# Other positions for the pieces of a chunked recurrence, and the weights' low parts all on VectorE

## The chip, the core and the metric

The kernel runs on one core of a Trainium2 chip. A core has five engines that run their own instruction streams side by side: PE (TensorE, matrix products), DVE (VectorE), ACT (ScalarE), POOL (GpSimd) and SP (SyncE, which only issues transfers here). The time is the device time of one execution in microseconds (us); of several runs the median counts. Before the change: median 640.99 us of 3 runs (640.5 to 645.92).

## The reference

Two parts follow each other. The first is a recurrence over 768 time steps, for 4 batches, 8 heads and a head size of 40, with a 40x40 state per head:

```python
for t in range(S):
    y[:, :, t] = np.einsum('bhd,bhde->bhe', rt, state)
    Sa = np.einsum('bhde,bhe->bhd', state, at)
    state_decay = state * wt[:, :, None, :] - np.einsum('bhd,bhe->bhde', Sa, bt)
    state = state_decay + np.einsum('bhd,bhe->bhde', vt, kt)
```

The second is an MLP on y, with heads side by side as x (4, 768, 320): h = gelu(x @ w_in); its two halves of 512 are u and v; v is normalised over its 512 columns and scaled by g_ln; v_s = w_sg @ v + b_sg mixes the 768 time steps; the result is x + (u * v_s) @ w_out. All is fp32.

## The kernel before

**Chunks.** The 768 steps are cut into 12 chunks c of 64, and each chunk into two halves f of the batches and heads. Inside a chunk the recurrence is a triangular system. What doesn't depend on the state is done ahead:

- *The gate* (gate_1 to gate_n): VectorE scans the decays (ex), makes at and, from a scan and a reciprocal, kb; PE turns kb over (kt, copied by ACT to kbt) and multiplies at with kb (ab); VectorE masks ab (at), ACT copies the negated part to nts.
- *The inversion* (inv_load, inv_in, inv_sub, inv_end, inv_turn, inv_back, inv_g, inv_x), once for several chunks: POOL substitutes row by row (tg, x), VectorE ends it (x), transposes (x1z, xt, n), PE and ACT form gp, gs, xp.

What depends on the state is the *chain*, for each c and f: chain1 (ru), chain2 (us), chain_t (tp), chain_u (ut), chain3 (sp, the new state), chain4 (pq) and chain5 (yp, the output), each with its post piece on VectorE or ACT (post1 rhsb, post2 vu, post3 sp and sc, post4 pqs, post5 yt). store5 writes yt out, load_main, load_vb (v, the tile vs), load_rv (rt and vut) fetch for a later chunk.

**Weights.** w_in is used as a high and a low fp32r part. The twelve weight steps k make these in six parts each: 0 loads (stg), 1 takes the size (ACT), 2 and 3 form the scale (DVE), 4 the parts (ACT: one Activate and the cast to wvh or wuh), 5 the low part, three tensor_tensor operations whose last writes wvl or wul. Part 5 is on POOL for the steps k in DECG, else on VectorE:

```python
steps[k] = self.split64(*self.weights_in()[k], HF // 2, self.G if k in DECG else self.V)
```

**Fillers.** While the chunks run, the v half of the MLP's first product is already made for finished time steps: fill_x (loads xf), fill_split (ACT, xfh), fill_low (POOL), fill_v (PE, hf), fill_out (ACT copies hv, SP stores it to hd). load_h reads it back later.

**What sets the order.** Each of these pieces has a position, a number worked out from tables at the head of the program: GATE, GATE0, CHAIN, CHAIN0, YC, YG, INV, BACK, BACK0 for the attention, MAIN_GAP and RV_GAP for the loads, DEC for the weights, FILL for the fillers, PF for reading v back. in_order (L128) sorts all pieces by position and holds a piece back only if a PSUM bank of its ring of six isn't free; then the pieces are issued in that order, each engine in its own queue, and no engine leaves its order. All instructions are issued by one helper, so that every row of the profile says L207. What starts when is decided on the chip, by semaphores. A position is no time: a table entry matters only where two pieces on the same engine change places.

After the chunks comes the MLP proper, batch by batch, up to the end.

Of the kernel before, what the change touches and what calls it, by code (L numbers as in the profile page):

```python
# [43 lines left out]
PER = 25.258  # L44
LATE = 2.5
STORE = 1.5
MAIN_GAP = (3.823, 5.231)
RV_GAP = (1.429, 5.124)
GATE = ((-101.908, -100.107, -99.028, -96.184, -97.801, -95.604, -92.188, -90.251, -93.577, -91.478, -91.765),
    (-93.068, -92.176, -89.578, -85.892, -88.462, -84.822, -80.052, -78.616, -83.325, -79.617, -81.192))  # L50
GATE0 = {(0, 0): (-50.0, (0, 0.6, 1.2, 2.0, 2.1, 3.5, 5.0, 6.2, 6.1, 10.6, 7.4)), (0, 1): (-43.168, (-4.513, -1.768,
# [6 lines left out]
CHAIN = ((-0.122, 2.573, 2.346, 4.973, 4.791, 6.367, 14.029, 15.925, 17.635, 7.581, 9.16, 11.953, 14.479, 16.712,  # L58
    19.293), (10.765, 12.016, 2.382, 3.709, 12.847, 14.479, 15.198, 19.282, 26.19, 15.086, 19.937, 24.082, 25.956,
    28.774, 31.466))  # L60
YC = (6.033, 31.49, 75.962, 101.266, 126.664, 152.164, 177.592, 203.193, 228.664, 254.164, 279.909, 305.328)
YG = (45.508, 65.508, 85.4, 105.4, 126.723, 152.223, 177.723, 203.223, 228.723, 254.223, 280.52, 303.785)
GATEE = {}
GROUPS = ((0,), (1,), (2, 3), (4, 5), (6, 7), (8, 9), (10, 11))
LAST = 2
NBANK = 6
INV = (-61.391, -53.031, -52.526, 0.739, -5.821, -4.877)
INV0 = {0: (-39.357, -31.7, -29.5, 0.443, -3.788, -2.8), 1: (-3.842, -2.4, -0.439, 0.265, 24.398, 26.261), 2: (19.888,
    26.888, 28.456, 0.0, 70.088, 70.788)}
CHAIN0 = {(0, 0): (0.0, 1.942, 2.468, 5.095, 5.152, 6.489, 14.151, 16.047, 17.757, 8.655, 9.521, 12.185, 14.84,  # L70
# [6 lines left out]
BACK0 = {0: (-2.477, -2.272, 2.034, -1.241, 0.905, 2.425, 4.594), 1: (-3.032, -0.637, -0.655, -1.796, -0.68, 1.87,  # L77
    4.322), 2: (-3.032, -0.036, -0.536, -1.677, 0.469, 1.989, 5.535)}
SUBV = ()
N2 = (1, 3)  # L80
KB = 2
BACK = (-4.003, -1.954, -2.561, -3.786, -2.662, 0.399, 2.058)
END_GT = 227.015
END_IW = 274.738
END_RING = 286.936
# [3 lines left out]
PIN = 227.025  # L89
DSTEP = ((-8.5, -1.0, 0.0, 0.7, 1.4, 2.4), (-8.5, -1.0, 0.0, 0.7, 1.4, 2.4))  # L90
DSTEPF = (-9.0, -0.5, 0.0, 0.7, 1.4, 2.4)
DEC = (10.0, 22.0, 34.0, 46.0, 58.0, 72.837, 235.802, 236.543, 248.778, 254.633, 260.025, 266.234)
GE = "VV"
FILL = ((-10.518, -5.255, 1.182, 5.082, 8.462), (3.438, 13.076, 15.947, 19.922, 22.61))
FILLG = True
LASTF = 5
PX = 309.28
# [1 line left out]
PV = 287.036  # L99
PS = 333.785  # L100
PL = 326.785
PF = (302.234, 311.634, 315.428, 323.94, 327.057)
PH = 9
FILLERS = ("v0", "v1", "v2", "v3", "v4")
FIRSTS = ("u1", "u0", "v0", "v1", "u2", "v2", "u3", "v3", "v4", "v5", "u4", "u5", "u6", "u7")
# [1 line left out]
    "v5", "o3", "o5", "o4", "u2", "u3", "u4", "u5", "u7", "u6")  # L107
SEQ_LAST = ("s1", "s2", "s0", "s3", "s4", "s5", "o0", "s6", "s7", "o1", "o2", "o3", "o5", "o4")
XS = 0
DECG = (1, 4)  # L110
DECE = "GGGGGGGG"
DENSE = 1000
DSTEPJ = (-1.1, 0, 0.2, 0.4, 0.6, 0.9)
# [107 lines left out]
def attention(tc, a, xd, flag, keep, ps, mlp=None):  # L221
# [4 lines left out]
    with ExitStack() as ctx:  # L226
# [419 lines left out]
        def at_(p, f, *args, **kw):  # L646
            pieces.append((p, f, args, kw))
# [9 lines left out]
        for c in range(NCH):  # L657
            for f in range(2):
                y, n = GATE0.get((c, f)) or (YG[c], GATE[f])
                at_(y + n[0], gate_1, c, f, 0)  # L660
# [10 lines left out]
                for h in range(2):  # L671
                    at_(y + n[5] + LATE + (MAIN_GAP[f] if h and c > 1 else 0), load_main, 2 * c + f + 2, h)
                z, n = YC[c], CHAIN0.get((c, f), CHAIN[f])
                for g, p in zip((chain1, post1, chain_t, post_t, chain2, post2, chain3, post3, copy3, chain_u, post_u, chain4, post4, chain5, post5), n):
# [4 lines left out]
                for x in range(2):  # L679
                    at_(z + n[13] + LATE + (RV_GAP[f] if x else 0), load_rv, c + 1, f, x)  # L680
            z = YC[c]
            for (g, *k), p in zip(((inv_back, 0), (inv_back, 1), (inv_back, 2), (inv_g,), (post_g,), (inv_x,), (post_x,)), BACK0.get(c, BACK)):
                at_(z + p, g, c, *k)
        for g in GROUPS:
            z, v = (0, INV0[g[0]]) if g[0] in INV0 else (YC[g[0]], INV)
            at_(z + v[0], inv_load, g)
# [39 lines left out]
class Mlp:  # L726
# [345 lines left out]
    def side(self):  # L1072

        def at(p, f, *args):
            plan.append((p, f, args))
# [5 lines left out]
        def wstep(k, i):  # L1081
            if i == 0:
                steps[k] = self.split64(*self.weights_in()[k], HF // 2, self.G if k in DECG else self.V)
            steps[k][i]()

        for k, p in enumerate(DEC):
            for i, d in enumerate(DSTEPF if k < 6 else DSTEP[k % 2]):
                at(p + d if k < 6 else max(PIN + 0.1, p + d), wstep, k, i)
        for k in range(LASTF):
            for b in range(B):  # L1090
                for f, p in zip((self.fill_x, self.fill_split, self.fill_low, self.fill_v, self.fill_out), FILL[1 - b % 2]):
                    n = 2 * k + 2 + (b + 1) // 2
                    at(YC[min(n, NCH - 1)] + PER * max(0, n - NCH + 1) + p, f, b, k)
        at(PO, self.open_out)
# [18 lines left out]
        at(PS, self.split_x, 0, 1)  # L1113
        for k, p in enumerate(PF[:LASTF]):
            at(p - PH, self.load_h, 0, k)
# [177 lines left out]
```

## Time and profile before

| | |
|---|---|
| median of 3 runs | 640.99 us |
| the profiled execution | 640.75 us, its span 639.0 us |
| mean granted clock of PE | 0.886 |
| PE busy | 537.8 us (84%) |
| DVE busy | 494.5 us (77%) |
| ACT busy | 368.9 us (58%) |
| POOL busy | 372.6 us (58%) |
| read from and written to HBM | 54.86 MB, 13.11 MB |

The span runs from the first to the last instruction of the profiled execution. No engine is busy throughout: each stage has its own limit, and so the share of a whole span says little. Roughly, the program is getting ready and inverting for chunk 0 until 62 us, is in chunks 0 to 2 until 160 us, in chunks 3 to 11 until about 390 us, and in the MLP from then on. Rows of a timeline give the start, the duration, the engine, the operation, the tile written and the tiles read with their forms, how many instructions stand together in the row, and in brackets the idle time before it with what ended that. "issue" there means that the engine waited for nothing the profile shows.

### The profile page before, as it was taken

The numbers are of one execution on the slowest core, as the hardware profiler recorded it, in microseconds if no ns is written. First come the engines' busy times: TensorE is split into PE (matmuls) and PEld (weight loads), VectorE is DVE, ScalarE is ACT, GpSimd is POOL, SyncE is SP. The second block draws the span as 40 slices with busy tenths as digits, with TensorE's granted clock in tenths as the row PEclk, the third lists the DMA queues.
The fourth block names the chain that finished last, engine by engine and source line by source line (L and its number), as shares of the span: only waits on it lengthen the run. The fifth ranks groups of instructions, "written<-read, shape, count | busy, mean of one in ns | idle before, by whom it ended". The sixth has DMA issues, their size and how long they took to land.

```text
span 639.0 us, 24143 instructions
## 1 busy us (share of the span) xinstructions
PE 537.8 (84%) x10158; PEld 487.1 (76%) x10158; DVE 494.5 (77%) x948; ACT 368.9 (58%) x817; POOL 372.6 (58%) x606
## 2 busy tenths in 40 slices
PE   6338876867998979889888897798999997999896
PEld 5228765766887868778777786688998997999796
DVE  7768899798688857878799655667689699788833
ACT  2334867367787876788767777365255334424510
POOL 3485858818856980895798443647443634533421
PEclk7758779668999997999988798698999999999899
DMA  6543335343454643542454455245014231512001
GB/s 195 142 115 98 102 77 124 83 125 90 118 141 134 166 127 93 137 134 86 125 144 122 116 155 145 87 126 181 27 59 147 76 118 39 186 57 75 19 12 56
DMA packets 56862, 69.63 MB, mean 109 GB/s; under 512 B 23752, under 2 KB 41800, under 8 KB 54728
## 3 DMA queue, kind: packets, MB, share of 16 engines
q1 hardware_dynamic: 56744, 67.99, 37.5%
q8 instruction: 82, 1.34, 1.0%
q14 instruction: 36, 0.29, 0.2%
HBM read 54.86 MB, written 13.11 MB: 106 GB/s over the span
## 4 chain that ended last, share of the span: by engine, by line
PE 39%; DVE 33%; ACT 9%; issue 9%; DMA 3%; POOL 3%; SPq 2%; ACTq 0%; DVEq 0%; POOLq 0%
PE sg L207 8%; DVE v L207 4%; PE yp L207 4%; PE kt L207 4%; PE ab L207 3%; PE hf L207 3%; DVE fixed L207 3%; PE op L207 3%; PE pq L207 2%; DVE p L207 2%; ACT nts L207 2%; DVE g L207 2%; PE sp L207 2%; DVE kb L207 2%; DVE stg L207 2%
## 5 line engine op out<-in xcount | busy, mean ns | idle before, releaser
L207 POOL TENSOR_TENSOR tg<-x,n 128x135 f32<-128x135 f32 (+25 forms) x203 | 104.5, 515 | 86.3 <-DVE n L207 62.7
L207 POOL TENSOR_TENSOR x<-x,tg 128x135 f32<-128x135 f32 (+25 forms) x203 | 108.8, 536 | 15.9
L207 PE MATMUL sg<-wsh,vh 128*128 128x384 f32 x192 | 64.4, 346 | 10.2 <-ACT wsh L207 3.6
L207 PE MATMUL sg<-wsl,vh 128*128 128x384 f32 x192 | 64.0, 351 | 0.1
L207 PE MATMUL sg<-wsh,vl 128*128 128x384 f32 x192 | 63.8, 351 | 0.0
L207 ACT ACTIVATE nts<-ab 32x512 f32<-32x512 f32 x96 | 46.4, 483 | 21.4 <-PE ab L207 20.1
L207 PE MATMUL kt<-ident,kb 128*128 128x128 f32 x192 | 35.5, 335 | 27.1 <-DVE fixed L207 19.4
L207 POOL TENSOR_TENSOR gx<-g,gy 128x384 fp32r<-128x384 f32 x30 | 31.5, 1060 | 40.5 <-ACT gy L207 40.5
L207 POOL TENSOR_TENSOR rs<-rs,mhalf 128x1 f32<-128x1 f32 x24 | 14.6, 614 | 66.9 <-DVE rs L207 66.9
L207 DVE TENSOR_TENSOR at<-ab,mask 64x512 f32<-64x512 f32 x48 | 31.9, 677 | 26.8 <-ACT nts L207 19.3
L207 PEld LDWEIGHTS kt<-ident,kb 128*128 128x128 f32 x192 | 26.3, 170 | 31.6 <-issue 25.5
L207 ACT CAST vh<-v 128x512 fp32r<-128x512 f32 x24 | 14.6, 619 | 57.7 <-DVE v L207 57.7
L207 PEld LDWEIGHTS sg<-wsh,vh 128*128 128x128 f32 x192 | 36.1, 190 | 12.9 <-ACT vh L207 5.2
L207 ACT CAST gy<-g 128x384 fp32r<-128x384 f32 x30 | 15.4, 513 | 50.7 <-DVE g L207 48.0
L207 PE MATMUL ab<-at,kb 64*64 64x64 f32 x1536 | 37.3, 255 | 8.6 <-DVE fixed L207 6.0
L207 PEld LDWEIGHTS ab<-at,kb 64*64 64x64 f32 x1536 | 32.9, 166 | 12.7 <-issue 8.5
L207 PE MATMUL yp<-pqs,kbt 128*64 128x64 f32 x768 | 35.9, 262 | 3.5 <-DVE pqs L207 3.3
L207 DVE SCALAR_TENSOR_TENSOR g<-sg,gl,bt 128x384 f32<-128x384 f32 x32 | 19.6, 612 | 24.4 <-PE sg L207 13.9
L207 PEld LDWEIGHTS sg<-wsh,vl 128*128 128x128 f32 x192 | 38.2, 200 | 0.0
L207 PE MATMUL pq<-rt,vut 40*64 40x64 f32 x1536 | 33.0, 231 | 6.1 <-ACT vut L207 3.8
L207 PEld LDWEIGHTS sg<-wsl,vh 128*128 128x128 f32 x192 | 37.8, 198 | 0.4 <-DVE wsl L207 0.4
L207 PEld LDWEIGHTS yp<-pqs,kbt 128*64 128x64 f32 x768 | 32.1, 173 | 7.0 <-DVE pqs L207 4.1
(161 smaller groups left out, 1577.2 us busy)
## 6 DMA issues: line engine op xcount, KB each, us to landing
main<-main SPq DMA_DIRECT2D x44, 321.4 KB
hd<-hv SPq DMA_DIRECT2D x20, 256.0 KB
v<-hd SPq DMA_DIRECT2D x20, 256.0 KB
vs<-vb SPq DMA_DIRECT2D x24, 160.0 KB
rt<-rt SPq DMA_DIRECT2D x48, 80.0 KB
vut<-vt SPq DMA_DIRECT2D x48, 80.0 KB
xd<-yt SPq DMA_DIRECT2D x96, 40.0 KB
ws<-seq_w SPq DMA_DIRECT2D x20, 192.0 KB
```

Of the source, the lines that this page charges most:

```text
L207: return self.tc.keep_in_program_order(f(*a, **k))
```

## The change

Position tables take other values, and DECG is empty, so that the low parts of weight steps 1 and 4 are made by VectorE and no longer by POOL. No instruction is added or left out otherwise, and no size changes. The diff, cut to the tables by which most of the moves come about:

```diff
-MAIN_GAP = (3.823, 5.231)
-RV_GAP = (1.429, 5.124)
+MAIN_GAP = (5.4, 4.3)
+RV_GAP = (1.75, 1.2)
...
-YG = (45.508, 65.508, 85.4, 105.4, 126.723, 152.223, 177.723, 203.223, 228.723, 254.223, 280.52, 303.785)
+YG = (45.508, 65.508, 85.508, 105.508, 126.831, 152.331, 177.831, 203.331, 228.831, 254.331, 279.831, 305.331)
...
-BACK = (-4.003, -1.954, -2.561, -3.786, -2.662, 0.399, 2.058)
+BACK = (-4.003, -1.37, -2.126, -3.202, 0.204, 0.399, 2.642)
...
-DEC = (10.0, 22.0, 34.0, 46.0, 58.0, 72.837, 235.802, 236.543, 248.778, 254.633, 260.025, 266.234)
+DEC = (10.0, 22.0, 34.0, 46.0, 58.0, 72.658, 235.802, 242.234, 248.778, 254.446, 260.025, 266.234)
...
-FILL = ((-10.518, -5.255, 1.182, 5.082, 8.462), (3.438, 13.076, 15.947, 19.922, 22.61))
+FILL = ((-10.151, 1.572, 2.299, 5.449, 8.327), (3.438, 13.076, 15.947, 19.922, 22.61))
...
-PF = (302.234, 311.634, 315.428, 323.94, 327.057)
+PF = (302.802, 308.64, 314.802, 323.685, 326.802)
...
-DECG = (1, 4)
+DECG = ()
```

GATE, GATE0, CHAIN, CHAIN0, YC, INV and BACK0 change in the same manner. In the listings that follow, a row is an instruction (or several alike, xN) in the order in which its engine gets it, and a number behind a name only tells one tile from the next.

PE in chunk 0, where the change has the chain's second sp and the ab of gate (3, 1) in another order. Before:

```order
 L207 MATMUL sp<-vu_125,kbt_104 64x40 x16
 L207 MATMUL ab_1153<-at_144,kb 64x64 x2
 L207 MATMUL ab_1154<-at_144,kb 64x64 x2
...
 L207 MATMUL sp<-vu_126,kbt_105 64x40 x16
 L207 MATMUL ut<-ident,vu_126 104x64 x8
```

With the change:

```order
 L207 MATMUL sp<-vu_125,kbt_104 64x40 x16
 L207 MATMUL sp<-vu_126,kbt_105 64x40 x16
 L207 MATMUL ab_1171<-at_144,kb 64x64 x2
 L207 MATMUL ab_1172<-at_144,kb 64x64 x2
```

The second sp moved in front of all of ab; nts on ACT reads ab.

VectorE, a little later, between the end of inversion 1 (x<-x,n) and the first scan (ex) of gate (4, 0); yt is the output of chunk 0's first half, stg and wvl belong to weight step 1:

```order
 L207 SCALAR_TENSOR_TENSOR x<-x,n 128x15 x2
 L207 SCALAR_TENSOR_TENSOR x<-x,n 128x16
+L207 TENSOR_TENSOR stg_1227<-stg_1227,stg_1207 128x256
+L207 TENSOR_TENSOR stg_1008<-stg_1008,wvh 128x256
+L207 TENSOR_TENSOR wvl<-stg_1008,stg_1227 128x256
 L207 SCALAR_TENSOR_TENSOR ex_135<-main_94,fixed_92 128x260
 L207 TENSOR_TENSOR yt<-yp_1231,ex_127 128x4x64
 L207 TENSOR_TENSOR yt<-yp_1232,ex_127 128x4x64
```

The three operations of the low part were POOL's before. The three of weight step 4 come to VectorE in the same way, behind the scans of gate (5, 1) and in front of the two at of gate (5, 0). POOL's queue loses six instructions and is otherwise as it was in these places.

PE in chunk 1, from xp of the inversion to us of the first half. Before:

```order
 L207 MATMUL xp<-xt_97,gs_117 32x32 x32
 L207 MATMUL yp_1552<-pqs,kbt_105 64x64 x2
 L207 MATMUL yp_1553<-pqs,kbt_105 64x64 x2
...
 L207 MATMUL tp<-ident,sc_119 128x128 x4
 L207 MATMUL kt_1588<-ident,kb 128x128 x4
 L207 MATMUL kt_1589<-ident,kb 128x128 x4
 L207 MATMUL tp<-ident,sc_118 128x128 x4
 L207 MATMUL us_1626<-rhsb_115,xt_97 64x40
```

With the change:

```order
 L207 MATMUL xp<-xt_97,gs_117 32x32 x32
 L207 MATMUL tp<-ident,sc_118 128x128 x4
 L207 MATMUL tp<-ident,sc_119 128x128 x4
 L207 MATMUL kt_1575<-ident,kb 128x128 x4
 L207 MATMUL kt_1576<-ident,kb 128x128 x4
 L207 MATMUL yp_1591<-pqs,kbt_105 64x64 x2
 L207 MATMUL yp_1592<-pqs,kbt_105 64x64 x2
```

yp moved behind both tp and both kt. On VectorE the matching yt moved behind the low part of weight step 2. There are more moves of this sort. On VectorE, yt of chunk 1's second half now stands between the two scans of gate (5, 0), and the low part of weight step 6 stands in front of step 7's size, fields and scale. On PE, in chunks 3 to 7, kt of gate (c+3, 1) goes in front of gp, and in chunks 3 to 11 the second sp goes in front of chain_u (ut). On ACT, in chunks 3 to 11, the copies xt and kbt go in front of gs, and step 7's size and parts go behind rhsb and vu of chunk 8's second half. On SP, the second half of a load of main goes behind load_vb, load_rv of the next chunk's second half goes right behind store5 and ahead of the fillers' store, and load_h comes earlier.

## Rows read from the trace of the kernel before

**Rows 1.** Busy time by stretches: each engine (rows), granted clock, DMA share, GB/s.

```profile
84.50:107.60 23.10, 15.68 (x444) 13.50 (x440) 22.67 (x42) 16.74 (x40) 17.06 (x31) 0.78 0.41 102
121.60:137.50 15.90, 9.60 (x256) 8.42 (x252) 14.98 (x35) 6.96 (x14) 8.28 (x15) 0.71 0.46 121
...
222.00:248.00 26.00, 20.24 (x561) 18.17 (x560) 15.92 (x34) 16.15 (x37) 15.56 (x27) 0.80 0.37 94
326.00:352.00 26.00, 21.55 (x567) 18.70 (x556) 25.05 (x50) 19.35 (x48) 21.94 (x35) 0.87 0.42 121
```

**Rows 2.** Timeline of PE in chunks 4 and 6: start, us, instructions, idle before.

```profile
197.77 0.58 PE L207 MATMUL xp<-xt,gs 64*32 64x32 f32 x43 [1.08 <-issue]
...
240.02 0.86 PE L207 MATMUL sp<-vu,kbt 128*64 128x40 f32 x11 [4.41 <-issue]
```

**Rows 3.** The page's DMA queues: packets, MB, share of 16 engines.

```profile
q8 instruction: 82, 1.34, 1.0%
```

**Rows 4.** Timeline of PE in chunk 0, 80 to 83 us.

```profile
80.68 1.16 PE L207 MATMUL ab<-at,kb 64*64 64x64 f32 x64
81.77 1.13 PE L207 MATMUL sp<-vu,kbt 128*64 128x40 f32 x32
```

**Rows 5.** Timeline of ACT, 81 to 85 us.

```profile
81.88 1.99 ACT L207 ACTIVATE nts<-ab 32x512 f32<-32x512 f32 x4 [1.34 <-PE ab L207]
...
84.84 0.40 ACT L207 CAST wvh<-stg 128x256 fp32r<-128x256 f32 x1
```

**Rows 6.** Timeline of VectorE at 84 us.

```profile
84.49 0.69 DVE L207 TENSOR_TENSOR_SCAN ex<-main,fixed 128x260 f32<-128x260 f32 x1
```

**Rows 7.** Tile stg, VectorE's low parts: least, median, longest duration in ns.

```profile
L207 DVE TENSOR_TENSOR stg<-stg,stg x4: 372/416/562, 69.4 to 144.4; 128x256 f32<-128x256 f32 x4
L207 DVE TENSOR_TENSOR stg<-stg,wvh x4: 464/732/904, 69.9 to 144.7; 128x256 f32<-128x256 f32 x4
L207 DVE TENSOR_TENSOR wvl<-stg,stg x4: 424/646/759, 70.5 to 145.2; 128x256 fp32r<-128x256 f32 x4
```

**Rows 8.** Timeline of POOL: where it takes up work after a pause.

```profile
90.59 0.64 POOL L207 TENSOR_TENSOR tg<-x,n 128x31 f32<-128x31 f32 x1 [3.34 <-DVE call L207]
...
144.64 0.24 POOL L207 TENSOR_TENSOR tg<-x,n 128x31 f32<-128x31 f32 x1 [13.06 <-DVE n L207]
```

**Rows 9.** Timeline of PE in chunk 1, 96 to 102 us.

```profile
96.96 1.44 PE L207 MATMUL yp<-pqs,kbt 128*64 128x64 f32 x32
...
101.09 0.66 PE L207 MATMUL kt<-ident,kb 128*128 128x128 f32 x4 [0.15 <-ACT xt L207]
```

**Rows 10.** Timeline of VectorE in chunk 1, 100 to 133 us.

```profile
100.75 0.73 DVE L207 TENSOR_TENSOR yt<-yp,ex 128x256 f32<-128x256 f32 x2
...
118.63 1.27 DVE L207 TENSOR_TENSOR_SCAN ex<-main,fixed 128x260 f32<-128x260 f32 x2
121.62 0.76 DVE L207 TENSOR_TENSOR yt<-yp,ex 128x256 f32<-128x256 f32 x2 [1.72 <-PE yp L207]
...
131.37 0.68 DVE L207 TENSOR_TENSOR at<-ab,mask 64x512 f32<-64x512 f32 x1 [0.32 <-ACT nts L207]
132.22 0.76 DVE L207 TENSOR_TENSOR yt<-yp,ex 128x256 f32<-128x256 f32 x2 [0.17 <-PE yp L207]
```

**Rows 11.** Timelines of VectorE and ACT in chunk 8, 313 to 315 us.

```profile
313.20 0.50 DVE L207 TENSOR_SCALAR cv<-stg 128x256 int32<-128x256 int32 x1
314.06 0.93 DVE L207 TENSOR_SCALAR cv<-cv 128x256 f32<-128x256 f32 x2 [0.35 <-ACT cv L207]
...
314.83 0.42 ACT L207 ACTIVATE cv<-cv 128x256 f32<-128x256 int32 x1
```

**Rows 12.** Groups by line: busy us, mean ns, idle before with its releasers.

```profile
L207 PE MATMUL gp<-x1z,nts 64*32 64x32 f32 x768 | 9.9, 203 | 4.9 <-DVE x1z L207 3.9 <-DVE at L207 0.6 <-issue 0.3
```

**Rows 13.** Timeline of ACT in chunk 4, 193 to 196 us.

```profile
193.25 1.49 ACT L207 COPY gs<-gp 32x256 f32<-32x256 f32 x4 [0.99 <-PE gp L207]
...
195.41 0.76 ACT L207 COPY kbt<-kt 128x320 f32<-128x320 f32 x2
```

More of the change, by code (lines that the diff above doesn't have):

```diff
@@ L46 @@
 STORE = 1.5
-MAIN_GAP = (3.823, 5.231)
-RV_GAP = (1.429, 5.124)
-GATE = ((-101.908, -100.107, -99.028, -96.184, -97.801, -95.604, -92.188, -90.251, -93.577, -91.478, -91.765),
-    (-93.068, -92.176, -89.578, -85.892, -88.462, -84.822, -80.052, -78.616, -83.325, -79.617, -81.192))
-GATE0 = {(0, 0): (-50.0, (0, 0.6, 1.2, 2.0, 2.1, 3.5, 5.0, 6.2, 6.1, 10.6, 7.4)), (0, 1): (-43.168, (-4.513, -1.768,
[6 rows of a table removed]
[L58 to L61, printed above, removed]
-YG = (45.508, 65.508, 85.4, 105.4, 126.723, 152.223, 177.723, 203.223, 228.723, 254.223, 280.52, 303.785)
+MAIN_GAP = (5.4, 4.3)
+RV_GAP = (1.75, 1.2)
+GATE = ((-101.908, -100.107, -99.028, -96.184, -97.801, -95.604, -92.188, -90.251, -93.577, -91.478, -91.823),
+    (-93.163, -92.271, -89.673, -85.987, -88.462, -85.151, -80.147, -78.616, -83.325, -79.712, -81.287))
+GATE0 = {(0, 0): (-50.0, (0, 0.6, 1.2, 2.0, 2.1, 3.5, 5.0, 6.2, 6.1, 10.6, 7.4)), (0, 1): (-43.168, (-2.368, -1.768,
[6 rows of a table added]
+CHAIN = ((-0.122, 1.82, 2.346, 4.973, 4.791, 6.367, 14.029, 15.925, 17.635, 7.581, 9.16, 12.063, 14.479, 16.712,
+    19.293), (10.879, 12.452, 2.818, 4.145, 13.283, 14.157, 15.198, 18.064, 26.304, 15.522, 18.922, 24.082, 26.07,
+    28.888, 30.883))
+YC = (6.033, 31.49, 75.962, 101.266, 126.664, 152.164, 177.592, 203.366, 228.664, 254.164, 279.909, 305.328)
+YG = (45.508, 65.508, 85.508, 105.508, 126.831, 152.331, 177.831, 203.331, 228.831, 254.331, 279.831, 305.331)
 GATEE = {}
@@ L66 @@
 NBANK = 6
-INV = (-61.391, -53.031, -52.526, 0.739, -5.821, -4.877)
+INV = (-61.319, -53.011, -50.525, 0.759, -5.801, -4.857)
 INV0 = {0: (-39.357, -31.7, -29.5, 0.443, -3.788, -2.8), 1: (-3.842, -2.4, -0.439, 0.265, 24.398, 26.261), 2: (19.888,
@@ L76 @@
     15.32, 18.186, 26.426, 16.386, 18.934, 24.094, 26.082, 28.9, 30.895)}
-BACK0 = {0: (-2.477, -2.272, 2.034, -1.241, 0.905, 2.425, 4.594), 1: (-3.032, -0.637, -0.655, -1.796, -0.68, 1.87,
-    4.322), 2: (-3.032, -0.036, -0.536, -1.677, 0.469, 1.989, 5.535)}
+BACK0 = {0: (-2.477, -2.272, 2.034, -1.241, 0.905, 2.425, 4.594), 1: (-3.032, -0.637, -0.655, -1.796, 0.425, 1.87,
+    3.993), 2: (-3.032, -0.036, -0.536, -1.677, 0.469, 1.989, 5.535)}
 SUBV = ()
```

18 rows, old and new, of tables (CHAIN0, GATE0) are left out of this document.

## The prediction

> **What bounds the kernel.** I read the busy table by stretches first, then the timelines of the engines that are full in them, then the tile view of the low parts, and last the waits that the profile names "issue". Up to about 62 us POOL's first inversion sets the pace, and from 435 us the MLP runs in an order that the change leaves alone; I put both at zero. Chunks 0 to 2 (78 to 160 us) are bound by VectorE: it is busy 22.67 of 23.10 us in one stretch and 14.98 of 15.90 in another [rows 1]. There every microsecond put on VectorE comes out at the end, unless a wait of VectorE takes it up. Chunks 3 to 10 repeat every 25 to 26 us, and PE is stopped now and then by waits that no engine ends, named "issue": 1.08 us in front of an xp, and once 4.41 us in front of an sp [rows 2], in a stretch whose granted clock is 0.80 [rows 1] (full speed, 1, is 2.4 GHz, and the lower level 1.2). I read these waits as instruction fetch: the queue that carries instructions as its kind moves 1.34 MB in 82 packets [rows 3], which is 16 KB each, and the long wait comes right behind a burst of loads. Last, 326 to 352 us is full on VectorE again, 25.05 of 26 us [rows 1].
>
> **The sum** is made against the profiled execution, 640.75 us (span 639.0); the median of the three runs shown is 640.99, so 0.2 us above.
>
> *Term 1, the low part of weight step 1, +2.8.* Its three operations go from POOL to VectorE, between the end of inversion 1 and the gate scan ex that now starts at 84.49 [rows 6]. The second of them reads wvh, and ACT's cast of it ends at 84.84 + 0.40 = 85.24. That cast stands behind the nts copies, which waited 1.34 us for PE's ab [rows 5]. PE now runs the second sp in front of this ab. That sp takes 1.13 us as a row, 1.1 with the rows' overlap [rows 4], so nts and cast come 1.1 later, and the cast ends at 86.3. Behind it two operations remain. Their least durations are 0.464 and 0.424 us, their medians 0.73 and 0.65, their longest 0.90 and 0.76 [rows 7]. I take the least, because POOL has nothing to do there until 90.59 (3.34 us of idle) [rows 8], and the slow end I lay to work beside POOL. So ex starts at 86.3 + 0.46 + 0.42 = 87.2 in place of 84.49: 2.7, and 2.8 with a hand-over. Bounds: 1.3 (three least durations, 0.372 + 0.464 + 0.424, no wait) and 3.5 (86.3 + 0.90 + 0.76 against 84.49). POOL gains nothing, since it stands idle behind the three anyway.
>
> The Trainium skill (SBUF — State Buffer, "SBUF: two separate sides") has VectorE and GpSimd share a pair of ports that one of them holds for a whole instruction while the other blocks. The spread from 0.46 to 0.90 us in rows 7 would fit that. By that rule alone, operations that each meet one of POOL's would be at the slow end, and the sum 0.7 us higher; it would be the fast end where POOL is idle.
>
> *Term 2, yp behind kt in chunk 1, +0.5.* PE now does both tp and both kt before this yp. The second kt starts at 101.09 and leaves PE half a microsecond later (0.66 as a row, pipelined), about 101.6; then yp, 1.44 us [rows 9], ends at 103.0. Now yt starts at 100.75, takes 0.73 [rows 10], and the low part of weight step 2 follows it, 1.8 by the medians [rows 7], up to 103.3. After the change the low part goes first and yt waits for yp: 103.0 + 0.73 = 103.75, 0.5 later. Bounds 0 (kt goes earlier) and 0.9 (all of us, behind yp, is late, and with it the next chain).
>
> *Term 3, the scans split by yt, +0.6.* Two scans ex (1.27 us) run together at 118.63, after which VectorE waits 1.72 us for yp until 121.62 [rows 10]. After the change one of them stands behind this yt, so half of 1.27 us leaves the idle time and lands on the path. Bounds 0 and 0.64.
>
> *Term 4, the low part of weight step 4, +0.7.* Three operations come in front of two at. The cast they need is done by then, and POOL is idle there until 144.64 (13.06 us) [rows 8], so they cost their least, about 1.2 [rows 7]. Two waits behind them take some up: 0.32 in front of the second at, 0.17 in front of yt [rows 10]. 1.2 − 0.5 = 0.7. Bounds 0 and 1.7 (1.8 by the medians, nearly nothing absorbed).
>
> *Term 5, weight steps 6 and 7, +1.2.* Now VectorE waits 0.35 us at 314.06 for step 7's size and goes on with that step; the product of step 6 comes later. After the change step 6 is finished first. VectorE is free at 313.20 + 0.50 = 313.7, but the product reads what ACT writes in the row at 314.83, up to 315.25 [rows 11]. Step 7's copy in front of that row goes away, but hv, which waits for PE, stands between, so I leave the row where it is. That is 1.55 us of waiting in place of 0.35, and the stretch behind is full [rows 1]. Bounds 0 (the 0.95 us free in 326 to 352 and slack in front take it) and 2.0 (a second such wait for step 7's parts).
>
> *Term 6, the steady chunks, 0.* In each, kt moves in front of gp, and ACT's copies xt, kbt, xt in front of gs. gp waits 3.9 us in all for x1z [rows 12], so kt can win at most that. Against it gs, now 193.25 to 194.74, comes behind three copies of which the kbt one takes 0.76 us [rows 13], some 2 us, and ends near 196.7. There xp is stopped by "issue" until 197.77 anyway [rows 2]: that wait covers both the gain and the loss. If that cover is gone, gs is later by more than kt is earlier, and each even chunk loses some tenths. Bounds −3.9 and +7 (rival (b)). The moves on SP's queue (main's second halves behind the load of v, rt and vut of the next chunk behind a store) leave each load in front of its first reader, as far as I could follow them; they can act by the burst alone, which is a rival.
>
> Sum: 2.8 + 0.5 + 0.6 + 0.7 + 1.2 + 0 = 5.8; 640.75 + 5.8 = **646.6 us**. All lower ends of terms 1 to 5 give +1.3, all upper ends +8.7, so this case's own range is 642 to 650.
>
> **Rivals.**
> (a) *Not slower: the 4.41-us wait goes.* Main's second half is loaded in the middle of the burst in front of it, and now comes behind the load of v. What decides is whether PE's next 16 KB arrive before PE runs dry, that is a wait near 240 us of under about 0.5. Gain: 4.4 us, and of the slow clock at most 0.20 × 26 = 5.2 more, of which I count half: 7. 646.6 − 7 = 640. For it: the place of the move. Against: the burst's bytes are the same.
> (b) *A second such wait.* The steady chunks have similar bursts, and one of them stopped PE for long, so a new order may as well make another: 646.6 + 7 = 653.6.
> (c) *kt in front of gp pays*, gs hidden: 646.6 − 3.9 = 642.7.
> (d) *The wait goes and VectorE's waits take up most of the additions*: 640.75 + 1.3 − 7 = 635, less with (c).
> The Trainium skill (Runtime: NRT & Kernel Launch, "Instruction fetch mechanics") says that an engine's program is refilled in blocks of 16 KiB by its sequencer's own queue, and that crossing a block is mostly hidden. The block size agrees with rows 3. By "mostly hidden", (a), (b) and (d) would have no cause and the sum would stand; the 4.41 us without a releaser speak against it here.
>
> **How the numbers follow.** Forecast 0.50, (a) 0.22, (b) 0.19, (c) 0.05, (d) 0.04. One per cent, about what a measurement of this kernel can tell from no change, is 634.6 to 647.4 around 640.99. The forecast lies just inside: of its 0.50 I put 0.28 inside and 0.22 above. Nearly all of (a), 0.21, and (c) are inside: same 0.54. Slower: 0.22 + 0.19 = 0.41. Faster: (d) and a tail of (a), 0.05. The range 637 to 654 takes in (a), (b) and (c) and leaves out (d) and the tails.
>
> **What the profile after would show.** Term 1: VectorE idle some 1.7 us until ACT's wvh, then operations of about 0.4 us, ex near 87.2. Term 2: yt waiting for PE's yp, some 3 us later than 103.0. Term 3: one ex before, one behind yt. Term 4: a low part in front of at, and no wait at at. Term 5: VectorE idle 1.2 to 1.6 us on ACT's cv. Term 6: gp with less wait for x1z, xp waiting for gs or "issue" in each even chunk. So chunk 2 should begin 4.6 us later than now, and the rest arise past 310 us. The prediction is wrong if the steady period changes: one long "issue" wait more or less weighs as much as all terms together.

## The result and the profile after

The change made the kernel slower by 0.59%: the ratio to the kernel before is 1.0059, 95% interval 1.0038 to 1.0081, or 3.8 us (2.4 to 5.2) of 641. The medians of 20 runs each are 643.36 us (640.76 to 649.25) and 641.22 (636.91 to 653.02). The forecast was 646.6, within 637 to 654. Single executions of one kernel scatter by several microseconds, and the profiled one of after is a long one, 647.37 us; the profile of before was an average one. So this pair of traces differs by 6.6 us, more than the kernels do. A second trace of each kernel follows further down; where it differs, the text says so.

| | before | after |
|---|---|---|
| profiled execution, its span | 640.75, 639.0 us | 647.37, 645.7 us |
| mean granted clock | 0.886 | 0.876 |
| DVE busy, instructions | 494.5 us, 948 | 496.5 us, 954 |
| POOL busy, instructions | 372.6 us, 606 | 368.7 us, 600 |

The stretches that answer to [rows 1] (same columns; the limits are set where the same work stands in the later trace):

```profile
84.50:112.20 27.70, 18.19 (x509) 16.14 (x499) 25.36 (x51) 19.36 (x44) 14.81 (x28) 0.72 0.32 84
126.00:141.00 15.00, 8.82 (x200) 7.78 (x200) 14.58 (x33) 6.67 (x14) 6.72 (x14) 0.66 0.40 98
...
222.00:250.00 28.00, 24.62 (x751) 21.88 (x753) 18.47 (x39) 20.60 (x46) 18.84 (x32) 0.88 0.45 124
330.00:356.00 26.00, 21.21 (x536) 18.55 (x536) 24.12 (x46) 18.35 (x46) 21.88 (x34) 0.80 0.43 127
```

VectorE is no longer full in the first stretch: 2.3 us are idle in it. In the third the granted clock is 0.88 where it was 0.80. Both are places that the prediction named.

**Term 1.** Timelines of PE, ACT and VectorE of after, which answer to [rows 4], [rows 5] and [rows 6]; the last line is VectorE's x in the trace of before:

```profile
80.69 3.09 PE L207 MATMUL sp<-vu,kbt 128*64 128x40 f32 x64
83.70 1.16 PE L207 MATMUL ab<-at,kb 64*64 64x64 f32 x64
...
84.90 1.97 ACT L207 ACTIVATE nts<-ab 32x512 f32<-32x512 f32 x4 [3.34 <-PE ab L207]
...
87.83 0.40 ACT L207 CAST wvh<-stg 128x256 fp32r<-128x256 f32 x1
...
85.41 0.69 DVE L207 SCALAR_TENSOR_TENSOR x<-x,n 128x15 f32<-128x15 f32 x3
87.96 0.43 DVE L207 TENSOR_TENSOR stg<-stg,stg 128x256 f32<-128x256 f32 x1 [1.86 <-ACT stg L207]
88.30 0.42 DVE L207 TENSOR_TENSOR stg<-stg,wvh 128x256 f32<-128x256 f32 x1
88.76 0.43 DVE L207 TENSOR_TENSOR wvl<-stg,stg 128x256 fp32r<-128x256 f32 x1
89.10 0.69 DVE L207 TENSOR_TENSOR_SCAN ex<-main,fixed 128x260 f32<-128x260 f32 x1
...
83.89 0.69 DVE L207 SCALAR_TENSOR_TENSOR x<-x,n 128x15 f32<-128x15 f32 x3
```

Both sp run in front of ab, ab waits for them, nts waits for ab (3.34 us, 1.34 before), the parts of step 1 wait for nts, and VectorE stands still for 1.86 us. From the start of x to that of ex it is 3.69 us; in this trace of before, ex began 0.60 after x (83.89 to 84.49 [rows 6]). That is +3.1 us in this pair; the second trace of before gives less (further down).

**Terms 2 and 3.** VectorE of after, chunk 1, against [rows 10], and PE's yp in front of the second yt:

```profile
106.55 0.71 DVE L207 TENSOR_TENSOR wvl<-stg,stg 128x256 fp32r<-128x256 f32 x1
107.19 0.74 DVE L207 TENSOR_TENSOR yt<-yp,ex 128x256 f32<-128x256 f32 x2
...
122.11 0.69 DVE L207 TENSOR_TENSOR_SCAN ex<-main,fixed 128x260 f32<-128x260 f32 x1
123.41 0.76 DVE L207 TENSOR_TENSOR yt<-yp,ex 128x256 f32<-128x256 f32 x2 [0.61 <-PE yp L207]
124.08 0.69 DVE L207 TENSOR_TENSOR_SCAN ex<-main,fixed 128x260 f32<-128x260 f32 x1
...
121.63 1.15 PE L207 MATMUL yp<-pqs,kbt 128*64 128x64 f32 x32
```

The first yt has no wait in front of it. The second waits 0.61 us, not 1.72, with one scan in front of it and not two; the yp that it reads took 1.15 us, and 1.97 before, at the lower clock.

**The long "issue" wait**, against [rows 2], is smaller:

```profile
242.79 1.89 PE L207 MATMUL sp<-vu,kbt 128*64 128x40 f32 x41 [1.61 <-issue]
```

And gp waits more for x1z in this kernel, not less ([rows 12]: 3.9 us in all):

```profile
L207 PE MATMUL gp<-x1z,nts 64*32 64x32 f32 x768 | 10.0, 203 | 9.3 <-DVE x1z L207 8.2 <-issue 1.1
```

### The profile page after: what moved, and what is told of

Its sections match the earlier page's. It is cut to its first block, busy times and chain, and to the rows that moved or that the text cites. A ratio compares the mean times of both kernels' runs of the same rounds, so it can differ in the third digit from the quotient of the medians.

```text
span 645.7 us, 24134 instructions
## 1 busy us (share of the span) xinstructions
PE 544.7 (84%) x10158; PEld 493.7 (76%) x10158; DVE 496.5 (77%) x954; ACT 370.3 (57%) x817; POOL 368.7 (57%) x600
## 3 DMA queue, kind: packets, MB, share of 16 engines
q8 instruction: 82, 1.34, 0.9%
## 4 chain that ended last, share of the span: by engine, by line
PE 36%; DVE 32%; ACT 10%; issue 9%; POOL 6%; DMA 5%; SPq 2%; DVEq 0%; ACTq 0%; POOLq 0%
PE yp L207 6%; PE sg L207 4%; DVE v L207 4%; PE hf L207 4%; PE sp L207 4%; PE ab L207 3%; DVE g L207 3%; DVE p L207 2%; PE pq L207 2%; DVE stg L207 2%; DVE cv L207 2%; PE kt L207 2%; DVE fixed L207 2%; DVE bs L207 2%; POOL tg L207 2%
## 5 line engine op out<-in xcount | busy, mean ns | idle before, releaser
L207 POOL TENSOR_TENSOR tg<-x,n 128x135 f32<-128x135 f32 (+25 forms) x203 | 105.9, 522 | 93.1 <-DVE n L207 47.6
L207 POOL TENSOR_TENSOR x<-x,tg 128x135 f32<-128x135 f32 (+25 forms) x203 | 106.8, 526 | 15.9
L207 POOL TENSOR_TENSOR vl<-v,vh 128x512 fp32r<-128x512 f32 x24 | 31.5, 1319 | 8.2 <-ACT vh L207 7.2
```

Of the source, the lines that this page charges most:

```text
L207: return self.tc.keep_in_program_order(f(*a, **k))
```

## The experiments

All are combinations of the two kernels' tables. Theory L says that the low parts on VectorE are the loss; its rival S, that the order in the steady chunks is.

**The low parts alone.**

```diff
 (kernel before)
-DECG = (1, 4)
+DECG = ()
```

> The kernel before with nothing but the low parts of weight steps 1 and 4 on VectorE; every other position as before. Theory L (the low parts are what costs): the cast of wvh is not late here (the second sp still stands behind ab), so VectorE waits about 0.6 us for it and then works 1.2 to 1.8 us: ex of gate (4, 0) some 1.6 to 2.1 us later than x's end, and 0.7 for step 4: +2.3 us, ratio 1.0036. Rival S (the order in the steady chunks is what costs, the low parts are taken up by later waits): below +0.7 us, ratio under 1.001. In either case POOL's inversions start no earlier.

Measured: 0.9961 (0.9930 to 0.9992). VectorE's rows in its profile:

```profile
87.53 0.68 DVE L207 SCALAR_TENSOR_TENSOR x<-x,n 128x15 f32<-128x15 f32 x3
88.12 0.42 DVE L207 TENSOR_TENSOR stg<-stg,stg 128x256 f32<-128x256 f32 x1
...
89.25 0.69 DVE L207 TENSOR_TENSOR_SCAN ex<-main,fixed 128x260 f32<-128x260 f32 x1
```

ex follows x by 1.72 us, 1.1 more than in the trace of before above, with no wait in front. The cast is ready, since sp still stands behind ab. These 1.1 us don't show in the time, which is, if anything, less. Theory L's ratio (1.0036) is missed and rival S's (under 1.001) holds; what made this kernel slightly faster isn't settled.

**The low parts taken back out of the change.**

```diff
 (kernel after)
-DECG = ()
+DECG = (1, 4)
```

> The changed kernel with the low parts of weight steps 1 and 4 back on POOL, all positions as changed. Theory L: 3.1 us (wait for wvh and the three operations, as measured in the changed kernel's profile between x's end and ex) and 0.7 go, so the ratio to the kernel before is 1.000 to 1.001. Rival S: it keeps at least two thirds of the loss, ratio 1.004 or more.

Measured: 0.9946 (0.9909 to 0.9983), faster than both kernels. The changed kernel itself, measured beside it, gave 1.0052, so the low parts cost 1.06% there, some 7 us, with an interval of about 3.5 us to either side. In the changed order it is the low parts that cost, as theory L says, but more than it said (1.000 to 1.001): VectorE's rows give at most 3.9 us, and where the rest arises isn't shown. In the order of before, the same six instructions cost nothing that the runs can tell.

**The positions at the start taken back.**

```diff
 (kernel after)
 GATE0, CHAIN0, BACK0: the values of the kernel before
```

> The changed kernel with GATE0, CHAIN0 and BACK0 as before: the second sp of chunk 0 stands behind ab again, the low parts stay on VectorE. If the late cast of wvh is what makes the low part of step 1 cost 2.9 to 3.1 us, VectorE's wait for ACT in front of it (1.86 and 1.65 us) falls under 0.6 us and ex follows x's start by 1.7 to 2.3 us, not 3.5 to 3.7; in time 1 to 2 us less than the changed kernel, ratio 1.001 to 1.006. If not, the wait stays over 1.4 us.

Measured: 0.9984 (0.9946 to 1.0022), against 1.0059 for the change: about 0.7% less, more than was expected. VectorE:

```profile
86.89 0.67 DVE L207 SCALAR_TENSOR_TENSOR x<-x,n 128x15 f32<-128x15 f32 x3
87.48 0.41 DVE L207 TENSOR_TENSOR stg<-stg,stg 128x256 f32<-128x256 f32 x1
...
88.60 0.69 DVE L207 TENSOR_TENSOR_SCAN ex<-main,fixed 128x260 f32<-128x260 f32 x1
```

The wait is gone, and ex follows x by 1.71 us, not 3.69: 2.0 us belong to the order of sp and ab. The instructions add 1.1 to the 0.60 of the first trace of before. These tables hold other moves too, and the runs don't divide the rest of the 0.7%.

**The order in the steady chunks alone.**

```diff
 (kernel before)
-BACK = (-4.003, -1.954, -2.561, -3.786, -2.662, 0.399, 2.058)
+BACK = (-4.003, -1.37, -2.126, -3.202, 0.204, 0.399, 2.642)
 GATE, CHAIN, YC, YG, INV: the values of the kernel after
```

> The kernel before with only the tables of the steady chunks changed (GATE, CHAIN, YC, YG, INV, BACK): kt in front of gp, xt and kbt in front of gs, the second sp in front of ut. Theory L: 0, between -1 and +1 us, ratio 0.998 to 1.002, gp waits less for x1z and xp more for gs or issue. Rival S: +3 to +4 us, ratio 1.005 to 1.006, the steady period 0.4 us longer per chunk.

Measured: 1.0146 (1.0106 to 1.0187), more than twice the whole change, and outside both expectations. gp does wait less for x1z, 2.4 us, as theory L said; the loss lies elsewhere. The long waits on PE, and gp:

```profile
244.06 1.72 PE L207 MATMUL sp<-vu,kbt 128*64 128x40 f32 x28 [4.35 <-issue]
...
276.90 1.38 PE L207 MATMUL sp<-vu,kbt 128*64 128x40 f32 x27 [3.10 <-issue]
...
L207 PE MATMUL gp<-x1z,nts 64*32 64x32 f32 x768 | 9.6, 199 | 3.0 <-DVE x1z L207 2.4 <-issue 0.6
```

Counted from 0, by PE's us and sp, the first of these waits is in chunk 5 and the second in chunk 6; the recorded texts call them 6 and 7.

SP's timeline in front of the second one:

```profile
268.50 0.30 SPq L207 DMA_DIRECT2D main<-main  x1
...
269.64 0.32 SPq L207 DMA_DIRECT2D main<-main  x1
271.20 0.47 SPq L207 DMA_DIRECT2D vs<-vb  x1
```

The second half of main now stands ahead of the load of v in this chunk as well. In the kernel before it stood behind it here, and ahead of it one chunk earlier, where the 4.41-us wait was. That gave theory F: the waits come from this order; its rival C says they are chance.

**The kernels once more, for a second profile.**

> The changed kernel unaltered, for a second profile. Whatever the theory, the ratio is 1.004 to 1.008. If the 4.23 us of issue in front of ru at 66 us and the 1.61 us in front of sp at 243 us belong to the change, they stand in this profile too within 0.5 us; if they are chance of an execution, they differ by 1 us or more. VectorE's wait for ACT in front of the low part of step 1 (1.86 us) is there within 0.3 us.

Measured: 1.0052 (1.0012 to 1.0093). VectorE's wait in front of the low part is 1.65 us, and ex follows x by 3.48. The issue wait in front of ru is there again, 4.25 us at 68 (2.80 and 2.87 in the two traces of before); the one near 242 is 1.06, 0.55 off, between the two marks that the expectation set.

> The kernel before unaltered, for a second profile. Theory F (the long issue waits come where the second half of a load of main is issued ahead of vs and xf, in one burst with the first half): the wait in front of sp near 240 us is here again, 1.5 to 4.5 us, and the one a chunk later, where the half stands behind vs, under 1.5. Rival C (the 4.41 us was chance): under 1 us at 240. Ratio 0.997 to 1.003.

Measured: 0.9989 (0.9954 to 1.0025). The waits:

```profile
244.24 0.86 PE L207 MATMUL sp<-vu,kbt 128*64 128x40 f32 x11 [2.49 <-issue]
...
272.94 0.49 PE L207 MATMUL sp<-vu,kbt 128*64 128x40 f32 x10 [1.49 <-issue]
```

The long one is there again, but 2.49 us and not 4.41; with the low parts alone on VectorE, where SP's order is the same, it is 1.52 in one trace. Its place is fixed, its size is not.

This trace also sets term 1 right. Here ex follows x by 2.12 us, not 0.60:

```profile
85.92 2.21 DVE L207 SCALAR_TENSOR_TENSOR x<-x,n 128x15 f32<-128x15 f32 x3
88.04 0.68 DVE L207 TENSOR_TENSOR_SCAN ex<-main,fixed 128x260 f32<-128x260 f32 x1
...
85.85 0.72 POOL L207 TENSOR_TENSOR stg<-stg,stg 128x256 f32<-128x256 f32 x1 [2.04 <-ACT stg L207]
```

POOL makes its low part of step 1 just beside these three x, and they take 0.70, 0.78 and 0.78 us. In the first trace POOL began at 85.01, behind them, and they took 0.24, 0.24 and 0.25, about as in both traces of the changed kernel. In two more traces (the loads alone, the steady order alone) an x beside this low part takes 0.64 to 0.73 us. In the eight traces of kernels that have this low part on POOL, ex follows x by 0.60 to 2.12 us. So on POOL, too, it can cost VectorE 1.5 us here, and the changed kernel's 3.69 and 3.48 us are 1.4 to 3.1 more. The 1.72 us of the low parts alone on VectorE lie within 0.60 to 2.12.

**The loads alone.**

```diff
 (kernel before)
-MAIN_GAP = (3.823, 5.231)
-RV_GAP = (1.429, 5.124)
+MAIN_GAP = (5.4, 4.3)
+RV_GAP = (1.75, 1.2)
```

> The kernel before with only MAIN_GAP and RV_GAP changed: in each even-half burst main's second half goes behind the load of v, and rt, vut of the next chunk's second half ahead of the fillers' store. Theory F: no issue wait of over 2 us in front of sp between 200 and 330 us, and 2 to 5 us less in all: ratio 0.992 to 0.997. Rival C: 0.998 to 1.002.

Measured: 0.9940 (0.9901 to 0.9979). The wait near 240 us is 1.12, and none in front of an sp from 200 to 330 us is longer. Theory F's numbers hold. The gain isn't shown to be this wait alone: PE's issue waits of over 0.3 us add up to 22.8 us until 430 us here, and to 21.7 and 20.5 in the two traces of before.

**Loads and steady order together; the change with the loads as before.**

> The steady chunks' tables and MAIN_GAP, RV_GAP changed, the rest as before. The steady tables alone gave 1.0146, with issue waits of 4.35 and 3.10 us in front of sp in chunks 6 and 7. Theory F: both fall below 2 us and the ratio to 1.002 to 1.008. Rival C: the ratio stays at 1.012 or more.

Measured: 1.0034 (0.9995 to 1.0073), 2.70 us near 240 and 0.45 a chunk later: the first is larger than was expected, the second and the time as theory F has them.

> The changed kernel with MAIN_GAP and RV_GAP as before. Theory F: an issue wait of 3 us or more in front of sp in at least one of chunks 4 to 8, and 3 to 7 us more than the changed kernel: ratio 1.010 to 1.016. Rival C: ratio 1.003 to 1.008.

Measured: 1.0171 (1.0108 to 1.0234). Both waits are back, and the time is a little over theory F's range:

```profile
246.84 1.40 PE L207 MATMUL sp<-vu,kbt 128*64 128x40 f32 x23 [3.79 <-issue]
...
277.85 1.40 PE L207 MATMUL sp<-vu,kbt 128*64 128x40 f32 x22 [3.14 <-issue]
```

The two tables of loads are worth 1.1% inside the change, and rival C falls.

**Only main's second half.**

```diff
 (kernel before, with the steady order)
-MAIN_GAP = (3.823, 5.231)
+MAIN_GAP = (5.4, 4.3)
```

> As the kernel with the steady chunks' tables alone (1.0146, issue waits of 4.35 and 3.10 us in front of sp in chunks 6 and 7), but with MAIN_GAP changed too: the only move is main's second half behind the load of v. Theory F (the place of that one load makes the long waits): both waits below 2.7 us, ratio 1.002 to 1.008, as with both load tables (1.0034). Rival V (it is rt and vut ahead of the fillers' store that helps): 1.012 or more.

Measured: 0.9987 (0.9954 to 1.0020), where the steady order without this edit had 1.0146. All pieces but the second halves of main stand in the same order in both kernels, and their traces show it: VectorE, ACT and POOL get the same instructions in the same order, and SP's queue differs by these halves alone (some move in chunks 0 to 2, too). Their place in SP's queue is worth 1.6%, ten microseconds, with an interval of about 3.4 to either side: more than either theory had. SP and PE in its chunk 5:

```profile
231.40 0.31 SPq L207 DMA_DIRECT2D main<-main  x1
...
234.10 0.47 SPq L207 DMA_DIRECT2D vs<-vb  x1
234.62 0.51 SPq L207 DMA_DIRECT2D main<-main  x1
...
238.25 1.37 PE L207 MATMUL sp<-vu,kbt 128*64 128x40 f32 x41 [1.61 <-issue]
```

What stood between is seen in the transfers of a stretch (by queue, and what was issued in it). In the kernel with the steady order alone, 234 to 241 us hold both halves of main and no packet of the queue q8, which carries instructions; its packet comes in 241 to 243, and PE goes on at 244.06:

```profile
q1 hardware_dynamic: 560, 1.25, 70.1%
...
issues: line engine op xcount, KB each, median us to landing
main<-main SPq DMA_DIRECT2D x2, 321.4 KB
...
q8 instruction: 1, 0.02, 4.2%
```

With main's second half behind v, the packet already comes in 235 to 237, beside the second half:

```profile
q8 instruction: 1, 0.02, 4.1%
...
main<-main SPq DMA_DIRECT2D x1, 321.4 KB
```

So PE's next 16 KB are served after both halves of main in the one order, and between them in the other. PE then stands still for 4.35 or 1.61 us. Packet by packet, with the steady order alone main's last one ends at 241.37 and q8's begins at 241.37; in the first trace of before it is 237.35 and 237.28.

That these waits are waits for instructions, the traces show: in the two of before, the two of the changed kernel and these two, PE has 96 "issue" waits of over 0.3 us until 430 us, and each ends 1.2 to 1.8 us after a packet of q8 has landed. The order of the loads isn't enough by itself. With the steady order alone main's halves also stand ahead of v at 181 and 209 us; there q8's packet comes at the start of the burst (183.0 and 211.3), and no issue wait follows in front of sp. As far as these traces tell, it takes both, the order and a packet that is due late in the burst.

The standstill cost more than its length, since PE came out of it at the lower of its two clocks (granted 0.50, which is 1.2 GHz). The 177 matmuls behind the wait, with the steady order alone and with main's half behind v:

```profile
244.00:252.10 8.10, 8.04 (x177) 7.60 (x177) 4.90 (x13) 3.36 (x6) 0.00 (x0) 0.50 0.07 20
...
238.20:243.10 4.90, 4.71 (x177) 4.35 (x176) 4.52 (x12) 3.98 (x8) 2.29 (x6) 1.00 0.14 29
```

From us in front of the wait to the next us it is 26.52 us (238.21 to 264.73) against 18.16 (235.14 to 253.30): 8.4 us of the ten, of which the difference of the two waits is only 2.7. The clock doesn't fall behind every wait: behind the 1.61 us here it stays at 1.00, behind the 1.61 of the changed kernel (at 242.79) it is 0.50 from 243.4 to 250.2 us.

**The fillers' loads out of the burst.**

```diff
 (kernel before, with the steady order)
-FILL = ((-10.518, -5.255, 1.182, 5.082, 8.462), (3.438, 13.076, 15.947, 19.922, 22.61))
+FILL = ((-1.0, 1.572, 2.299, 5.449, 8.462), (3.438, 13.076, 15.947, 19.922, 22.61))
```

> As the kernel with the steady chunks' tables alone, but FILL's first row moves the fillers' loads xf of the odd batches (and their split on ACT) half a chunk later, out of the burst in which main's second half stands ahead of v; main stays there. Theory B (it is the bytes queued in front of PE's program): the waits in front of sp in chunks 6 and 7 fall to 2 us or less, and a new wait may come in the other half, where xf now stands; ratio 1.003 to 1.012. Rival M (only main's own place counts): both waits stay over 2.5 us and the ratio over 1.012.

Measured: 1.0327 (1.0279 to 1.0374). Both waits stay, 4.35 and 2.54 us, though 192 KB of xf are out of the burst: theory B falls, and rival M holds. It is not the bytes behind v that count, but what stands ahead of it. Why the time grew by another 1.8% isn't settled; the move also sends the fillers' other pieces to new places.

**The two parts that were faster, together.**

```diff
 (kernel before)
+MAIN_GAP = (5.4, 4.3); RV_GAP = (1.75, 1.2); DECG = ()
```

> The kernel before with MAIN_GAP, RV_GAP changed and the low parts on VectorE, all else as before: the two parts that were faster by themselves (0.9940 and 0.9961). If they add up: 0.988 to 0.994. If the low parts alone were a lucky set of issue waits and cost what VectorE's rows say (1.1 + 0.7 us), 0.995 to 0.999.

Measured: 0.9947 (0.9904 to 0.9989), like the loads alone (0.9940), and between the two ranges. The low parts add nothing and cost nothing here that the runs can tell. It beats both kernels, as do the loads alone and the change with the low parts on POOL (0.9946); the runs don't tell these three apart.

## Why the prediction was right, and where it wasn't

The time lay in the range and on the forecast side, 3.8 us more against 5.8. The sum came near for reasons that are partly others than those given, and so partly by luck.

- *Term 1 (+2.8) had the mechanism right.* sp in front of ab delays nts, the cast and the low part. The wait was forecast at 1.7 us and was 1.86 and 1.65. The operations took their least durations (0.42 and 0.43 us beside an idle POOL). The Trainium skill's rule on shared ports (SBUF — State Buffer, "SBUF: two separate sides") gives the same end there. The size is +3.1 us against the first trace of before and +1.6 or +1.4 against the second. What the term had at nothing is that POOL's low part slows VectorE's x beside it (0.70 to 0.78 us each, not 0.24), a cost that goes away with the move.
- *Term 2 (+0.5) was nothing.* at in front of the low part came 4.61 us later than before (104.16 against 99.55), call behind yt 4.58 later (107.85 against 103.27); the second pair of traces agrees (3.70 us from the one to the other, 3.71 before). tp and kt ran earlier, in time that PE had spent waiting, and yp was done when yt was reached. That was its lower bound.
- *Term 3 (+0.6) is open.* From the first ex to call it took 3.66 us before (118.63 to 122.29) and 2.69 after (122.11 to 124.80), which is −1.0. In the second pair it took 1.97 (122.40 to 124.37) and 2.68 (122.96 to 125.64), which is +0.7, as forecast. I took VectorE's wait of 1.72 us for yp as given, and the second trace of before doesn't have it. The longer stretch, from call behind the first yt to this call, is shorter after the change in both pairs: 19.02 and 17.58 us before, 16.95 and 16.70 after. An "issue" wait in front of pq stands in it both times before (1.79 us at 110.80, 1.97 at 114.49) and in neither trace after, so this gain may be the order's.
- *Term 4 (+0.7) held*: from call to call 10.60 us before (122.29 to 132.89), 11.45 after (124.80 to 136.25), +0.85; in the second pair 10.94 and 11.71, +0.8.
- *Term 5 (+1.2) was nothing.* VectorE came to this place 5.35 us later and from a wait of 5.67 us for yp, so ACT was done first:

```profile
315.75 0.76 DVE L207 TENSOR_TENSOR yt<-yp,ex 128x256 f32<-128x256 f32 x2 [5.67 <-PE yp L207]
...
318.65 0.57 DVE L207 TENSOR_SCALAR cv<-stg 128x256 int32<-128x256 int32 x1
319.33 0.65 DVE L207 TENSOR_TENSOR cv<-cv 128x256 f32<-128x256 f32 x1
...
328.67 0.75 DVE L207 TENSOR_TENSOR yt<-yp,ex 128x256 f32<-128x256 f32 x2
```

From yt to yt it is 12.92 us, against 13.13 before (310.40 to 323.53); in the second pair 13.62 and 14.20. This is rival (d)'s idea that waits take additions up.
- *Term 6 (0) is the step that failed*, and the sum didn't show it. The steady order alone costs 1.46%, with main's second half ahead of v in chunk 6 too, and the place of these halves takes all of it off: that is rival (b), a second long wait, priced at 7 us and measured at 9. The load tables take 1.1% off in the change, and 1.6% come off by the place of main's second halves alone in the steady order: that is rival (a), also priced at 7. Both happened. I had held them to be alternatives, each with its own chance, and reckoned the order at zero because an "issue" wait near xp covered it. kt in front of gp did lessen gp's wait for x1z where the steady order stands alone (2.4 us, against 3.9 and 5.8 before), but with main's halves behind v, where it is 2.2, the time is that of before (0.9987). In the changed kernel gp's wait is 8.2 and 8.3 us, and 2.2 with the positions at the start taken back, so kt isn't what lengthens it.
- The Trainium skill (Runtime: NRT & Kernel Launch, "Instruction fetch mechanics") calls the crossing of a block "mostly hidden". By count this trace agrees: of 69 packets of q8 between 60 and 430 us in the kernel before, 18 came so late that PE waited over 0.3 us. By time it doesn't: the place of a load beside these packets decided over one per cent.

Terms 1 to 5 as measured make 3.1 + 0 − 1.0 + 0.85 − 0.2 = 2.75 us in the first pair and 1.4 + 0 + 0.7 + 0.8 − 0.6 = 2.3 in the second, not 5.8. From x to the call that ends term 4 the changed kernel takes 1.8 us more in the first pair (50.84 against 49.00) and 1.3 in the second (50.66 against 49.39), where terms 1 to 4 had 4.6. So the additions were overrated, and parts that stood at zero moved more time than the whole change, in both directions. Which places hold the rest of the 3.8 us isn't shown; DEC, FILL and PF were not taken alone with the change's values.

## What to carry to other kernels

Read a wait that the profile gives to no engine as a possible wait for instructions, and look at what was queued in front of that queue's next packet: here the cure was the place of the second halves of a load, 321 KB each. Price such a wait with the clock that follows it. Where an operation is moved to a full engine, what it waits for can cost more than what it takes (2.0 against 1.1 us here), and what it cost that engine from its old place goes away. One trace of each kernel isn't enough where executions scatter: a second one turned the sign of a term. Two effects that a forecast holds for alternatives may both happen; take each part alone before believing a sum that fits.

## What the runs showed of the hardware

PE's instruction packet of 16 KB waited behind two loads of 321 KB and not behind 192 KB of smaller rows beside them: 4.35 us of standstill with the smaller ones, and still 4.35 with them out of the burst. The same wait in the same program measured 4.41 and 2.49 us in two executions. Behind the 4.35 us PE's granted clock was 0.50 over 8.1 us, and 177 matmuls took 8.10 us and not 4.90. Three operations on VectorE took 0.70 to 0.78 us each beside three of POOL, and 0.24 to 0.25 without them.
